# A branch on TensorE in front of the down step of the late expert tiles

## The chip, the core and the metric

One core of one Trainium2 chip runs the whole program. The metric is the device time of one execution, in microseconds. Its engines are TensorE (PE in the profile; PEld is its loading of stationary operands), VectorE (DVE), ScalarE (ACT), GpSimd (POOL) and SyncE (SP). Each engine has a sequencer of its own (PEldq, ACTq and so on in the rows), which takes the instructions of that engine in program order, hands products and vector work on to the engine and carries out register loads, branches and waits on semaphores itself.

## What is computed

```python
X = rfft(x, axis=1)                       # x: (8, 2496, 256)
Yr = Xr @ w_r - Xi @ w_i + b_r ; Yi = Xr @ w_i + Xi @ w_r + b_i
Y = softshrink(Yr, 0.01) + 1j * softshrink(Yi, 0.01)
y = irfft(Y, axis=1).reshape(19968, 256)
logits = y @ w_gate                        # 8 experts
e = argmax(logits) ; g = softmax(logits)[e]
out[token] = g * (relu(y[token] @ w1[e]) @ w2[e])      # w1[e]: 256 x 1024, w2[e]: 1024 x 256
```

Each of the 19,968 tokens goes to one expert. With the inputs of the reference the eight experts get 2254, 2696, 2453, 2444, 2626, 2443, 2081 and 2971 tokens; this is counted from the reference on its own inputs, and is no reading of a trace.

## The kernel before

The first part of the program (the transforms, the mixing, the routing) is not touched. Each routed token is written into a DRAM buffer, `xs_dram`, in which every expert has its own stretch of rows. The second part takes the tokens in tiles of 256 rows (`TT`) of one expert. `tab0`, made when a good half of the tokens is routed, names the first 20 tiles (`EARLY`); `tab1`, made at the end by `table(1)`, names the others: expert by expert, all tiles that this expert still has. The tokens of an expert fill whole tiles only by chance, so an expert's last tile is moved back until it ends with the expert's last row. Its first rows then repeat rows of the tile before. How many they are is `lap`, and `table(1)` makes from it `drop`, which for each late tile and each of its 256 rows is 0, or a large number for a repeated row; added to the row's place in the output it puts that row out of bounds, and it is not written. All 256 rows of the tile are computed nevertheless.

`experts_rest` calls `step(t)` for the tiles 7 to 81, one after the other, with `up(t)` and `down(t)`:

- `up`: hidden layer of the tile, transposed, 1024 x 256, in four groups `ph` (`f2`). Every fp32 product is made of three in the rounded type fp32r: high times high, low times high, high times low. That is 48 products of 128 x 128 by 256 columns (L1143). ACT makes `hh` (relu, rounded, L1148) and DVE `hl` (what the rounding left, L1149) from each group.
- `down`: output of the tile in two halves `h` of 128 rows, each with its own bank `po` of PSUM. `product(..., wide=True)` is hh against the 512 columns of w2's high and low part (L1183, 8 for each half), `wide=False` is hl against the 256 columns of the high part (L1185, 8 for each half). In tiles 7 to 80 all 16 wide ones come first, the halves in turn, then the 16 narrow ones, the halves in turn; in tile 81 (`final`) one half follows the other.
- `give(h)`: ACT scales the low part (`part`, L1189), DVE adds it up to `o` (L1190), POOL scatters the 128 rows to the output (L1192).

`split1(t+1)` and `split2(t+1)` load a flag from the table into registers of ACT and DVE, and where the next tile has another expert, a branch on these two engines makes the high and low parts of the new w1 (L1075, L1076) and w2 (L1081, L1082). The other engines meet such a branch only as a jump from one block of the program to the next (UNCONDITIONAL_BRANCH). `experts_rest` starts with a register load on all engines (`live`, L1243) and ends with a branch of all engines on it (L1247), which decides on three more tiles; with these inputs they are not needed.

The order on ACT and DVE is that of the code; on PE it is as stated above. The instructions of a tile are written out for every tile, so PE's program is a straight line of some 170 instructions a tile, a product and the load of its stationary operand being two.

Of the kernel before, what the change touches and what calls it, by code (L numbers as in the profile page):

```python
# [13 lines left out]
I32 = mybir.dt.int32  # L14
AF = mybir.ActivationFunctionType
ALU = mybir.AluOpType
# [13 lines left out]
TT = 256  # L30
# [3 lines left out]
EARLY = 20  # L34
# [66 lines left out]
class Kernel:  # L101
# [41 lines left out]
    def open_inverse(self, st, pst):  # L143
        nc, nb = self.nc, self.nb
        cp = self.cp
        self.ident = cp.tile([128, 128], F32, name="ident")
        make_identity(nc, self.ident)
        self.carry_b = cp.tile([117, E], BF16, name="carry_b")
        self.base = cp.tile([128, E], F32, name="base")
        nc.vector.memset(self.carry_b, 0.0)  # L150
        self.ones_b = cp.tile([117, 128], BF16, name="ones_b")
        nc.vector.memset(self.ones_b, 1.0)
        self.unit = cp.tile([128, E], F32, name="unit")
        nc.vector.memset(self.unit, 1.0)
        self.used = cp.tile([128, E], F32, name="used")
        nc.vector.memset(self.used, 0.0)
        self.tabs = [cp.tile([1, 4, n], I32, name=f"tab{i}") for i, n in enumerate((EARLY + 4, self.nt - EARLY + 1))]
        self.drop = cp.tile([128, self.nt - EARLY + 1, 2], I32, name="drop")
        self.tcol = cp.tile([128, 5], F32, name="tcol")

        k = self.k = self.pool(st, "k", 1)
        self.wi = self.pool(st, "wi", 3)
        self.rt = self.pool(st, "rt", 1)
        self.psi = self.pool(pst, "psi", 2, space=PSUM)
        self.wg = k.tile([128, 2, 32], F32, name="wg")
        nc.vector.memset(self.wg, 0.0)
        self.gar = k.tile([120, 117], F32, name="gar")
        self.gh = k.tile([120, 128], F32R, name="gh")[:, 0:117]
        self.gl = k.tile([120, 128], F32R, name="gl")[:, 0:117]
        self.ids = k.tile([117, nb, G], I32, name="ids")  # L170
        self.score = k.tile([117, G, E], F32, name="score")
        self.ltri = k.tile([117, 117], BF16, name="ltri")
        self.hot = k.tile([117, 3, GH * E], F32, name="hot")
        self.ltri_f = self.hot.rearrange("p i n -> p (i n)")[:, 0:117]
        self.rank = k.tile([117, E, GH], BF16, name="rank")
        self.keep = k.tile([117, E, GH], F32, name="keep")
        self.ex = k.tile([117, GH, E + 1], F32, name="ex")
        self.mark = k.tile([1, 1], F32, name="mark")
        self.zf = [k.tile([128, 5288], F32, name=f"z{i}") for i in range(2)]
        self.skip(k, 32)  # L180
        self.zs = [z[:, 0:5280].rearrange("p (c n a) -> p c n a", c=2, n=66) for z in self.zf]
# [710 lines left out]
    def table(self, last):  # L892
        nc, rt = self.nc, self.rt
# [5 lines left out]
        for _ in range(6 if last else 0):  # L899
            yield "wait"  # L900
        p = self.psi.tile([128, 512], F32, tag="yo", name="pn")
# [6 lines left out]
                                op0=ALU.add, op1=ALU.mult)  # L908
# [29 lines left out]
        if not last:  # L938
            nc.vector.tensor_scalar(out=st0, in0=st0, scalar1=-1.0, scalar2=float(self.early),
                                    op0=ALU.mult, op1=ALU.add)  # L940
# [19 lines left out]
        p = self.psi.tile([128, 512], F32, tag="yo", name="pq")  # L960
# [5 lines left out]
        if last:  # L966
            lap = rt.tile([128, 128], F32, name="lap")
            nc.vector.tensor_copy(lap, fin[:, 3:4].broadcast_to((128, 128)))
            for _ in range(7):
                yield  # L970
            p = self.psi.tile([128, 512], F32, tag="yo", name="pl")
            nc.tensor.matmul(p[:, 0:128], lap, self.ident, start=True, stop=True)
            for h in range(2):
                nc.vector.tensor_scalar(out=self.drop[:, :, h], in0=p[:, 0:self.drop.shape[1]], scalar1=tcol[:, 3 + h:4 + h],
                                        scalar2=float(OOB), op0=ALU.is_gt, op1=ALU.mult)

# [181 lines left out]
    def down(self, t):  # L1160
        tc, nc = self.tc, self.nc
        hh, hl = self.hs.pop(t)
        w2 = self.h2
        xr = self.xrs.pop(t)
        if t >= self.early:
            row = self.w2p.tile([128, 2], I32, tag="row", name="row", bufs=2)
            nc.vector.tensor_tensor(out=row, in0=xr.bitcast(I32)[:, :, 1], in1=self.drop[:, t - self.early, :],
                                    op=ALU.add)
            at = [row[:, h:h + 1] for h in range(2)]
        else:  # L1170
            at = [xr.bitcast(I32)[:, h, 1:2] for h in range(2)]
        o = self.w2p.tile([128, 2, D], F32, tag="o", name="o", bufs=2)
        if t == self.early:
            self.skip(self.w2p, 160)

        def bank():
            return (self.psb.tile([128, 512], F32, tag="o", name="po") if self.psb else
                    self.psi.tile([128, 512], F32, tag="u", name="po", bufs=4))

        def product(p, h, f, wide):  # L1180
            hs = slice(h * 128, (h + 1) * 128)
            if wide:
                nc.tensor.matmul(p, hh[:, f, hs], w2[:, f].rearrange("p a d -> p (a d)"), start=f == 0, stop=False)  # L1183
            else:
                nc.tensor.matmul(p[:, :D], hl[:, f, hs], w2[:, f, 0, :], start=False, stop=f == 7)  # L1185

        def give(p, h):
            part = self.w2p.tile([128, D], F32, tag="part", name="part", bufs=2)
            nc.scalar.activation(part, p[:, D:], AF.Copy, scale=xr[:, h, 0:1])  # L1189
            nc.vector.scalar_tensor_tensor(out=o[:, h, :], in0=p[:, :D], scalar=xr[:, h, 0:1], in1=part,  # L1190
                                           op0=ALU.mult, op1=ALU.add)
            i = nc.gpsimd.indirect_dma_start(  # L1192
                out=self.out[:, :], out_offset=bass.IndirectOffsetOnAxis(ap=at[h], axis=0),
                in_=o[:, h, :], in_offset=None, bounds_check=self.ntok - 1, oob_is_err=False)
            if t or h:
                tc.declare_no_dep(i.ins, group="out", reason="every token is in one tile only")
            tc.add_to_no_dep_group("out", i.ins)

        if self.psb and t < self.final:
            ps = [bank() for _ in range(2)]  # L1200
            for wide in (True, False):
                for f in range(8):
                    for h in range(2):
                        product(ps[h], h, f, wide)
                if wide:
                    self.split1(t + 1)
                    yield
            for h in range(2):
                give(ps[h], h)
            yield  # L1210
            return
        for h in range(2):
            p = bank()
            for wide in (True, False):
                for f in range(8):
                    product(p, h, f, wide)
                if wide and t < 2:
                    yield
            if not h:
                self.split1(t + 1)  # L1220
            give(p, h)
            yield

    def step(self, t):
        if t + 4 <= self.nt - RARE:
            self.load(t + 4)
        yield from self.up(t, self.upright(t + 1))
        yield from self.down(t)
# [50 lines left out]
```

## Time and profile before

| | us |
|---|---|
| median of 3 runs (lowest, highest) | 1471.36 (1469.13, 1471.93) |
| the profiled execution | 1460.86 |
| its span, first to last instruction | 1459.1 |
| PE busy in the span | 1435.5 |
| DVE, ACT, POOL busy | 926.3, 769.0, 475.0 |

The profile is of one execution, which took 10.5 us less than the median of the runs without a profile. Matmuls are pipelined: the next one starts long before the one before is reported as ended, so what a product costs in a stream is the distance from start to start. The sequencers' instructions are not counted as busy; for an instruction that waits or is late, the reader looks at its start.

### The profile page before, as it was taken

Reading aid. Unit: us, or ns where it says so; the run is one execution under the profiler, and the core shown is the slowest. Engines: PE = TensorE matmul, PEld = TensorE weight load, DVE = VectorE, ACT = ScalarE, POOL = GpSimd, SP = SyncE. Lnnn points to the kernel's source line nnn. Section 1 sums busy time; section 2 is a strip of 40 time slices with the busy share of each in tenths; the row PEclk is TensorE's granted clock in tenths of the full one; section 3 lists DMA queues with packets and bytes.
Section 4 is the critical chain, followed back from the end, with each engine's and each line's share of the span. In section 5 each row is a group of like instructions: output and inputs, shape, how many; then the busy total and the mean of one; then the engine's idle time right before and its main releaser. Section 6 shows DMA issues by size and latency. Waiting matters only on the chain. (4 is left out here: it accounts for less than half of the span.)

```text
span 1459.1 us, 34933 instructions
## 1 busy us (share of the span) xinstructions
PE 1435.5 (98%) x10547; PEld 1311.2 (90%) x10548; DVE 926.3 (63%) x1959; ACT 769.0 (53%) x1540; POOL 475.0 (33%) x586
## 2 busy tenths in 40 slices
PE   8999999999999999999999999999999999999997
PEld 4889898898989878899999999999999999999996
DVE  3788898988998886555565545464445445445443
ACT  2688787787877764443444434343434334334332
POOL 2042566657574454334311111111111111111121
PEclk9999999999999999999999999999999999999999
DMA  7875565656554333444342323233223223232210
GB/s 200 239 229 137 144 177 162 171 162 180 163 155 147 83 98 92 106 125 118 96 117 74 101 59 99 72 87 81 68 55 97 49 56 99 48 85 68 48 50 21
DMA packets 193733, 161.20 MB, mean 110 GB/s; under 512 B 127847, under 2 KB 164367, under 8 KB 193308
## 3 DMA queue, kind: packets, MB, share of 16 engines
q1 hardware_dynamic: 173364, 112.58, 30.7%
q0 software_dynamic: 20160, 46.20, 9.3%
q8 instruction: 87, 1.43, 0.4%
q14 instruction: 122, 1.00, 0.2%
HBM read 241.20 MB, written 66.37 MB: 211 GB/s over the span
## 5 line engine op out<-in xcount | busy, mean ns | idle before, releaser
L1143 PE MATMUL ph<-xh,h 128*128 128x256 f32 x1312 | 363.0, 277 | 0.0
L1143 PE MATMUL ph<-xl,h 128*128 128x256 f32 x1312 | 362.7, 276 | 0.0
L1143 PE MATMUL ph<-xh,l 128*128 128x256 f32 x1312 | 362.7, 276 | 0.0
L1183 PE MATMUL po<-h,hh 128*128 128x512 f32 x1312 | 313.6, 390 | 0.8 <-DVE h L1082 0.5
L1192 POOL DMA_INDIRECT out<-o,row x124 | 121.7, 981 | 556.7 <-DVE o L1190 534.4
L1149 DVE SCALAR_TENSOR_TENSOR hl<-ph,hh 128x512 fp32r<-128x512 f32 x328 | 226.0, 689 | 109.2 <-ACT hh L1148 94.6
L1183 PEld LDWEIGHTS po<-h,hh 128*128 128x128 f32 x1312 | 239.4, 188 | 47.3 <-ACTq L1087 1.5
L1148 ACT ACTIVATE hh<-ph 128x512 fp32r<-128x512 f32 x328 | 194.0, 599 | 159.0 <-PE ph L1143 120.4
L1190 DVE SCALAR_TENSOR_TENSOR o<-po,xr,part 128x256 f32<-128x256 f32 x156 | 68.7, 480 | 311.8 <-ACT part L1189 309.5
L1189 ACT ACTIVATE part<-po,xr 128x256 f32<-128x256 f32 x156 | 65.9, 471 | 344.9 <-PE po L1185 317.9
L1143 PEld LDWEIGHTS ph<-xh,h 128*128 128x128 f32 x1312 | 246.4, 188 | 0.5 <-issue 0.3
L1143 PEld LDWEIGHTS ph<-xl,h 128*128 128x128 f32 x1312 | 246.5, 188 | 0.0
L1143 PEld LDWEIGHTS ph<-xh,l 128*128 128x128 f32 x1312 | 246.3, 188 | 0.2
L877 POOL DMA_INDIRECT xs_dram<-yb,pos x176 | 177.5, 1009 | 59.7 <-issue 44.7
L1185 PEld LDWEIGHTS po<-h,hl 128*128 128x128 f32 x1312 | 167.0, 188 | 6.9
L1185 PE MATMUL po<-h,hl 128*128 128x256 f32 x1312 | 169.1, 279 | 0.0
L475 DVE SCALAR_TENSOR_TENSOR y<-v,r 64x256 f32<-64x256 f32 x320 | 133.6, 417 | 5.7 <-ACT r L469 0.6
L495 ACT COPY z<-pv 128x256 f32<-128x256 f32 x160 | 93.9, 709 | 0.1
L408 PE MATMUL pb<-bm,t 128*128 128x128 f32 x640 | 88.3, 282 | 4.9 <-DMA t<-spec_dram 4.9
L408 PEld LDWEIGHTS pb<-bm,t 128*128 128x128 f32 x640 | 79.8, 194 | 14.4 <-issue 5.6
L491 PE MATMUL pv<-bi,y 128*128 128x128 f32 x640 | 86.9, 277 | 2.3 <-DVE y L475 2.2
L816 POOL COPY mark<-y 1x1 f32<-1x1 f32 x72 | 25.8, 358 | 193.2 <-DVE y L475 192.5
(209 smaller groups left out, 2464.7 us busy)
## 6 DMA issues: line engine op xcount, KB each, us to landing
r<-moe_w SPq DMA_DIRECT2D x672, 128.0 KB
r<-moe_w SPq DMA_DIRECT2D x166, 512.0 KB
xq<-xs_dram SPq DMA_DIRECT2D x332, 64.0 KB
t<-spec_dram SPq DMA_DIRECT2D x160, 128.0 KB
spec_dram<-ae SPq DMA_DIRECT2D x77, 240.0 KB
x<-x SPq DMA_DIRECT2D x38, 384.0 KB
x<-x SPq DMA_DIRECT2D x38, 84.0 KB
xs_dram<-yb,pos POOLq DMA_INDIRECT x176, 2.9
```

The costliest lines, as they stand in the source:

```text
L408: nc.tensor.matmul(p[:, c, :, kp, :], t[:, kp, c * 128:(c + 1) * 128], self.bm[:, 2 * s + kp, :], start=True, stop=True)
L475: nc.vector.scalar_tensor_tensor(out=y[q * 64:q * 64 + 64, kp, :], in0=u[h, q, :], scalar=LAM, in1=r[h, q, :], op0=ALU.add, op1=ALU.min)
L491: nc.tensor.matmul(p[:, c, kp, :, :], y[:, kp, c * 128:(c + 1) * 128], self.bi[:, 2 * s + kp, :], start=True, stop=True)
L495: nc.scalar.copy(self.zs[b % 2][:, c, 0:NB, 4 * s:4 * s + 4].rearrange("p n a -> p a n"), p[:, c].rearrange("p a r n -> p (a r) n"))
L877: i = nc.gpsimd.indirect_dma_start(out=self.xs[:, :], out_offset=bass.IndirectOffsetOnAxis(ap=pos[:n, g:g + 1], axis=0), in_=y[:n, g, :], ...
L1143: nc.tensor.matmul(p[:, i, :], a[:, c, f * 128:(f + 1) * 128], v[:, c, :], start=m == 0, stop=m == 5)
L1148: nc.scalar.activation(hh[:, s, :], p, AF.Relu)
L1149: nc.vector.scalar_tensor_tensor(out=hl[:, s, :], in0=p, scalar=0.0, in1=hh[:, s, :], op0=ALU.max, op1=ALU.subtract)
L1183: nc.tensor.matmul(p, hh[:, f, hs], w2[:, f].rearrange("p a d -> p (a d)"), start=f == 0, stop=False)
L1185: nc.tensor.matmul(p[:, :D], hl[:, f, hs], w2[:, f, 0, :], start=False, stop=f == 7)
L1190: nc.vector.scalar_tensor_tensor(out=o[:, h, :], in0=p[:, :D], scalar=xr[:, h, 0:1], in1=part, op0=ALU.mult, op1=ALU.add)
L1192: i = nc.gpsimd.indirect_dma_start(out=self.out[:, :], out_offset=bass.IndirectOffsetOnAxis(ap=at[h], axis=0), in_=o[:, h, :], in_offset=N ...
```

## The change

`table(1)` makes one more row, `full`: 1 for a late tile with fewer than 128 repeated rows, else 0. In tiles 20 to 80, `down` loads it into a register of PE and branches. Where it is 1, PE does the same products as before, the narrow ones now half by half. Where it is 0, the whole first half of the tile is repeated rows, which are not written: a single wide product fills the first half's bank with numbers that no one needs, the second half is done, and 7 wide and 8 narrow products of the first half are left out. The 8 narrow products of the second half stand behind the branch, for both. In tiles 7 to 19 and 81 nothing is changed.

```diff
--- before.py
+++ after.py
@@ -156,6 +156,7 @@
         nc.vector.memset(self.used, 0.0)
         self.tabs = [cp.tile([1, 4, n], I32, name=f"tab{i}") for i, n in enumerate((EARLY + 4, self.nt - EARLY + 1))]
         self.drop = cp.tile([128, self.nt - EARLY + 1, 2], I32, name="drop")
+        self.full = cp.tile([1, self.nt - EARLY + 1], I32, name="full")
         self.tcol = cp.tile([128, 5], F32, name="tcol")
 
         k = self.k = self.pool(st, "k", 1)
@@ -973,6 +974,8 @@
             for h in range(2):
                 nc.vector.tensor_scalar(out=self.drop[:, :, h], in0=p[:, 0:self.drop.shape[1]], scalar1=tcol[:, 3 + h:4 + h],
                                         scalar2=float(OOB), op0=ALU.is_gt, op1=ALU.mult)
+            nc.vector.tensor_scalar(out=self.full, in0=p[0:1, 0:self.full.shape[1]], scalar1=float(TT // 2), scalar2=1.0,
+                                    op0=ALU.is_lt, op1=ALU.mult)
 
 
 
@@ -1198,13 +1201,25 @@
 
         if self.psb and t < self.final:
             ps = [bank() for _ in range(2)]
-            for wide in (True, False):
+            if t >= self.early:
+                with self.whole(t) as cmp:
+                    for f in range(8):
+                        for h in range(2):
+                            product(ps[h], h, f, True)
+                    for f in range(8):
+                        product(ps[0], 0, f, False)
+                with cmp.Else():
+                    nc.tensor.matmul(ps[0], hh[:, 0, 0:128], w2[:, 0].rearrange("p a d -> p (a d)"), start=True, stop=True)
+                    for f in range(8):
+                        product(ps[1], 1, f, True)
                 for f in range(8):
-                    for h in range(2):
-                        product(ps[h], h, f, wide)
-                if wide:
-                    self.split1(t + 1)
-                    yield
+                    product(ps[1], 1, f, False)
+            else:
+                for wide in (True, False):
+                    for f in range(8):
+                        for h in range(2):
+                            product(ps[h], h, f, wide)
+            self.split1(t + 1)
             for h in range(2):
                 give(ps[h], h)
             yield
@@ -1220,6 +1235,11 @@
                 self.split1(t + 1)
             give(p, h)
             yield
+
+    def whole(self, t):
+        i = t - self.early
+        return self.tc.If(self.nc.values_load(self.full[0:1, i:i + 1], engines=(mybir.EngineType.PE,),
+                                              min_val=0, max_val=1) > 0)
 
     def step(self, t):
         if t + 4 <= self.nt - RARE:
```

The first place is PE between the last product of `up` and the first of the next `up`, in a tile that takes the branch. Here `po` is the output bank, `ph` a group of the hidden layer, h_8031 and h_8032 are the same buffer, w2's parts, and `full` the new row. Before:

```order
L1143 MATMUL ph<-xl_12753,h_7217 128x256
L1095 UNCONDITIONAL_BRANCH
L1183 MATMUL po<-h_8031,hh 128x512 x16
L1185 MATMUL po<-h_8031,hl 128x256 x16
L1087 UNCONDITIONAL_BRANCH
L1143 MATMUL ph<-xh_12961,h_7217 128x256
```

After, with the line numbers of the changed code:

```order
L1146 MATMUL ph<-xl_12755,h_7218 128x256
L1241 TENSOR_LOAD full
L1241 ISA x2
L1098 UNCONDITIONAL_BRANCH
L1205 COMPARE_AND_BRANCH
L1186 MATMUL po<-h_8032,hh 128x512 x16
L1188 MATMUL po<-h_8032,hl 128x256 x8
L1205 UNCONDITIONAL_BRANCH
L1212 MATMUL po<-h_8032,hh 128x512
L1186 MATMUL po<-h_8032,hh 128x512 x8
L1205 UNCONDITIONAL_BRANCH
L1188 MATMUL po<-h_8032,hl 128x256 x8
```

The 16 narrow products fall into 8 before the jump and 8 behind the branch; a register load, two register instructions and a comparison come in front of the wide products; the four rows from the first L1205 jump to the second are the other side of the branch (9 products), which a tile with `full` = 1 jumps over.

The second place is ACT at the end of a tile, from the last two hidden groups to the branch on a new expert (`tab` is the table, h the high part of w1). Before:

```order
L1114 CAST xh_12752<-xf 128x512
L1148 ACTIVATE hh<-ph 128x512 x2
L1055 TENSOR_LOAD tab_75
L1055 ISA x2
L1087 COMPARE_AND_BRANCH
L1075 CAST h_7217<-r_7215 128x512
L1075 CAST h_7217<-r_7216 128x512
```

After:

```order
L1117 CAST xh_12754<-xf 128x512
L1151 ACTIVATE hh<-ph 128x512 x2
L1058 TENSOR_LOAD tab_75
L1058 ISA x2
L1205 UNCONDITIONAL_BRANCH
L1090 COMPARE_AND_BRANCH
L1078 CAST h_7218<-r_7216 128x512
L1078 CAST h_7218<-r_7217 128x512
```

ACT gets one jump a tile in front of that comparison, and its work stands as before; DVE, POOL and SP get the same one jump a tile, 61 in all on each.

## Rows read from the trace of the kernel before

**Rows 1.** Page, busy time of each engine, share of the span and instructions

```profile
PE 1435.5 (98%) x10547; PEld 1311.2 (90%) x10548; DVE 926.3 (63%) x1959; ACT 769.0 (53%) x1540; POOL 475.0 (33%) x586
```

**Rows 2.** Windows: busy us of each engine (instructions), granted clock, DMA share, GB/s

```profile
core 0: us, PE busy (x) PEld busy (x) DVE busy (x) ACT busy (x) POOL busy (x), PEclk, DMA share, GB/s
...
775.90:1444.43 668.53, 668.53 (x4883) 630.55 (x4881) 334.09 (x607) 263.06 (x485) 119.72 (x122) 1.00 0.27 69
...
1104.67:1115.63 10.96, 10.96 (x83) 10.34 (x81) 8.82 (x17) 6.87 (x14) 1.96 (x2) 1.00 0.53 137
```

**Rows 3.** Timeline of PE in tile 50: start, us, engine, line, operation

```profile
1104.67 3.79 PE L1183 MATMUL po<-h,hh 128*128 128x512 f32 x16
...
1108.29 2.04 PE L1185 MATMUL po<-h,hl 128*128 128x256 f32 x16
...
1110.18 0.28 PE L1143 MATMUL ph<-xh,h 128*128 128x256 f32 x1
...
1115.63 0.61 PE L1183 MATMUL po<-h,hh 128*128 128x512 f32 x2
```

**Rows 4.** Timeline of PE in tile 81, one half after the other

```profile
1444.43 1.97 PE L1183 MATMUL po<-h,hh 128*128 128x512 f32 x8
...
1446.24 1.10 PE L1185 MATMUL po<-h,hl 128*128 128x256 f32 x8
...
1447.18 2.02 PE L1183 MATMUL po<-h,hh 128*128 128x512 f32 x8
```

**Rows 5.** Timelines of ACT (tiles 50, 69) and DVE (tile 50)

```profile
1104.87 0.60 ACT L1148 ACTIVATE hh<-ph 128x512 fp32r<-128x512 f32 x1 [0.76 <-PE ph L1143]
...
1105.66 2.19 ACT L1075 CAST h<-r 128x512 fp32r<-128x512 f32 x4 [0.20 <-DMA xq<-xs_dram]
...
1313.92 2.19 ACT L1075 CAST h<-r 128x512 fp32r<-128x512 f32 x4 [0.21 <-ACT hh L1148]
...
1105.50 0.69 DVE L1149 SCALAR_TENSOR_TENSOR hl<-ph,hh 128x512 fp32r<-128x512 f32 x1
...
1106.34 2.50 DVE L1076 TENSOR_TENSOR l<-r,h 128x512 fp32r<-128x512 f32 x4
```

**Rows 6.** By source line, PE's sequencer (PEldq): duration ns, first and last start; one weight load

```profile
L1243 PEldq TENSOR_LOAD <-tab x1: 486/486/486, 624.8 to 624.8; - x1
...
L1143 PEldq EVENT_SEMAPHORE  x1: 51/51/51, 625.4 to 625.4; - x1
...
L1183 PEldq EVENT_SEMAPHORE  x1: 51/51/51, 1102.6 to 1102.6; - x1
...
1104.55 3.48 PEld L1183 LDWEIGHTS po<-h,hh 128*128 128x128 f32 x16
...
L1143 PEldq EVENT_SEMAPHORE  x2: 51/51/51, 1107.9 to 1110.9; - x2
```

**Rows 7.** The same for ACT's sequencer, and ACT's own work then

```profile
L1055 ACTq TENSOR_LOAD <-tab x1: 279/279/279, 940.5 to 940.5; - x1
...
L1087 ACTq COMPARE_BRANCH  x1: 45/45/45, 941.0 to 941.0; - x1
...
L1087 ACTq EVENT_SEMAPHORE  x1: 17/17/17, 941.2 to 941.2; - x1
...
L1095 ACTq COMPARE_BRANCH  x1: 45/45/45, 935.1 to 935.1; - x1
...
934.95 0.84 ACT L1189 ACTIVATE part<-po,xr 128x256 f32<-128x256 f32 x2 [4.84 <-PE po L1185]
```

**Rows 8.** Program's end: PE's one branch, last products, instruction queue from 1447.5 to 1448

```profile
L1247 PEldq COMPARE_BRANCH  x1: 3352/3352/3352, 1447.0 to 1447.0; - x1
...
L1185 PE MATMUL po<-h,hl x8: 276/280/285, 1449.0 to 1449.9; 128*128 128x256 f32 x8
...
q8 instruction: 1, 0.02, 11.1%
```

**Rows 9.** Timeline of DVE at the second table

```profile
600.78 0.47 DVE L974 TENSOR_SCALAR drop<-pl,tcol 128x66 int32<-128x66 f32 x2
```

## The prediction

> **What bounds the kernel now.** I read the page first: PE is busy for 98% of the span, the next engine, DVE, for 63% [rows 1]. The windows say it of the stage that the change touches: from 775.90 (down of tile 20) to 1444.43 (down of tile 81) PE is busy for all 668.53 us, with a granted clock of 1.00, which is the upper of its two levels, while DVE and ACT are busy for half or less [rows 2]. So here the time is the sum of PE's products and nothing else. The timeline of tile 50 gives their price in a stream, start to start [rows 3]: 16 wide ones from 1104.67 to 1108.29, 3.62 us or 0.226 each; 16 narrow ones from there to 1110.18, 1.89 us or 0.118 each; the 48 products of up from there to 1115.63, 5.45 us or 0.113 each. A tile is 10.96 us, and the second window shows it as all busy [rows 2].
>
> **What the skip saves.** Which tiles are skipped follows from the data. From the counts of tokens, lap is 256 times the number of tiles less the count: 50, 120, 107, 116, 190, 117, 223 and 101 for the experts 0 to 7. Only 190 and 223 reach 128: the last tile of expert 4 and that of expert 6. The other 59 of the 61 tiles get the branch for nothing. The trace shows where the two are. Counting 10.96 us a tile from tile 81, the down at 1104.67 is that of tile 50, and in it ACT splits the w1 of a new expert, at 1105.66; the next but one such split stands at 1313.92 [rows 5], 19 tiles on, and experts 5 and 6 have 10 and 9 tiles. So the skips are in tiles 50 and 69.
>
> A skipped down is 1 + 8 wide and 8 narrow products: 9 x 0.226 + 8 x 0.118 = 2.98 us in place of 5.51, a saving of 2.53 us, or 5.06 us for both. That 8 products in a row to one bank cost no more than in turn is shown by tile 81, where 8 wide ones take 1446.24 - 1444.43 = 1.81 us (0.226 each) and 8 narrow ones 1447.18 - 1446.24 = 0.94 (0.118) [rows 4]; so the new order of the narrow ones is free in the 59 tiles too.
>
> Is PE itself what ends last in the shortened tile? The next up, with the new expert's w1, would start at 1104.67 + 2.98 = 1107.65 in place of 1110.18. It needs the first low part of w1, the first of four DVE operations from 1106.34 (2.50 us for four, so it is done at about 1107.0), the second after three products, at 1108.0 (done at about 1107.6), the other two 24 products later [rows 5]. hh's last group is done at 1104.87 + 0.60 = 1105.5, and hl's last at about 1106.2; the skipped down wants them at 1106.3 and 1107.4 [rows 5]. All of it is covered by 0.2 us or more; if that cover were gone, the price is at most the end of the last DVE operation, 1108.84, less 1107.65, some 1.2 us a skip. I take 0.
>
> **What the branch costs.** For PE's array nothing is added; the question is its sequencer, which has to carry out a register load, two register instructions, a jump and a comparison before it can hand on the first wide product. It runs ahead of the array: the wait in front of that product (L1183) is carried out at 1102.6, and the load for the product starts at 1104.55: 1.95 us ahead, or 17 products. In front of the next up the wait at 1107.9 is 2.2 us ahead of 1110.18 [rows 3, 6]. In the same position, right behind a tile's products, the one register load that PE has now (L1243) starts at 624.8 and takes 486 ns; the wait behind it is at 625.4, 0.6 us after the start, and no work of PE is held up by it [rows 6]. For the other instructions ACT has the nearest rows: from the start of its register load at 940.5 to the first instruction on the far side of a taken branch, at 941.2, 0.7 us pass, of which the load is 279 ns [rows 7]. With PE's own load the chain is 0.5 + 0.4 = 0.9 us. PE's wait takes 51 ns where ACT's takes 17; if all small instructions of PE were three times as slow, the chain would be 0.5 + 3 x 0.4 = 1.7 us. Both ends are below 1.95, so I cost the branch at 0: it is hidden by the 17 products already handed on. Behind it come the wide products, at 0.226 us each twice as long as those of up, so the sequencer gets its lead back within the same down.
>
> [...]
>
> Of a tile that jumps over the other side (some 24 instructions), the jump falls behind 8 narrow products, where the lead is larger still. On ACT, DVE, POOL and SP there is one jump a tile more; ACT and DVE are idle for half of the stage [rows 2], so that I cost it at nothing. The operation that makes `full` has one partition and 66 columns; `drop`, 128 partitions and 66 columns, takes 0.24 us each [rows 9], so 0 to 0.24 us, once, beside PE's work: 0.
>
> **The sum.** Profiled execution: 1460.86 - 5.06 = 1455.8 us, its span 1454.0. The median of the runs stands 10.5 us above the profiled execution; I carry that difference over: 1471.36 - 5.06 = 1466.3 us, 0.34% faster. The measurement can tell about 0.2% from no change, that is 2.9 us, so the gain survives if the 59 idle branches cost less than some 35 ns each.
>
> **Rivals.**
>
> 1. The branch empties PE. The only compare-and-branch that PE has now, behind tile 81, starts at 1447.0 and lasts 3352 ns. It ends just when the last product does, whose start is at 1449.9 and which takes 0.28 us [rows 8]. If the comparison waits there until the array is empty, it does so 61 times. Each costs the 0.28 us of the last product less the 0.113 to the next start, then about 0.15 to the branch's end, 0.1 for the wait and the handing on, and 0.12 between the load and the product (1104.55 to 1104.67 [rows 3, 6]): 0.45 to 0.6 us, 27 to 37 us in all. Less 5, this is 1493 to 1503; I would take 1500. Slower than before from 83 ns a branch on. Against it: ACT's comparison at 935.1 takes 45 ns in the midst of work that runs from 934.95 to 935.79 [rows 7], and the register load and jumps of PE do not wait for the array [rows 6]. And there is another cause for the 3352 ns: a block of instructions (0.02 MB) is fetched after 1447.5, out of turn [rows 8]; that branch jumps over three tiles' program, some 500 instructions, to a place that was not there yet.
>
> [...]
>
> 3. The chain is longer than the lead. If PE's sequencer needs 2.1 to 2.4 us for it, 0.15 to 0.45 us stand open in each of 61 tiles: 9 to 27 us, less 5: 1475 to 1494, say 1483.
>
> 4. The skip does not happen, or the next tile waits as long as was saved: 1471.4.
>
> **How the numbers follow.** Hidden branch, two skips: 0.67. The branch empties PE: 0.12. Jumps that miss: 0.06. Chain too long: 0.11. No skip: 0.04. The forecast is 1466.3; with 2.8 us below it, the distance from the lowest to the highest run shown, the range starts at 1463.5. To hold 8 in 10, it has to take in the missing jumps, no skip and the shorter half of the too long chain: 0.67 + 0.06 + 0.04 + 0.05; it ends at 1483. By its own, the forecast's range is 1463.5 to 1469. Faster by over 0.2%: 0.64 (the hidden case, less a little for scatter and the 0.2 us margins). Within 0.2%: 0.12 (that rest, no skip, most of the missing jumps). Slower: 0.24 (emptied PE, long chain, the worst of the jumps).
>
> **What would show it.** In the profile after, PE busy from tile 20 to tile 81 without a gap, that stretch 5.1 us shorter; tiles of 10.96 us, but 8.43 us for tiles 50 and 69, with 9 wide and 8 narrow products. On PE's sequencer, 61 comparisons of 0.1 us or so, and the wait in front of the wide products still ahead of them, by about 1 us. [...] I am wrong if PE has idle time of more than 0.08 us a tile there, or if no tile is short.

## The result and the profile of the changed kernel

| | before | changed |
|---|---|---|
| median of 4 runs (lowest, highest), us | 1470.95 (1469.13, 1471.93) | 1489.23 (1486.20, 1490.06) |
| ratio, 95% interval | | 1.0122 (1.0104 to 1.0140) |
| the profiled execution, us (its span) | 1460.86 (1459.1) | 1490.06 (1488.2) |

The changed kernel is 18.3 us slower; 5 us faster was forecast, and the time lies above the range. The profiled execution of before was 10 us under its own median, that of the changed kernel is not, so the two are compared stage by stage and not by their spans. What sets two executions of the same work apart lies ahead of this stage: in the profile of before, the down step of tile 7 starts at 633.39, in that of e3 below, which took 1468.81 us and has the same tiles of 10.96 us from there on, at 641.30. Its cause is not shown.

The page of the changed kernel still shows PE as what bounds it, as in [rows 1]:

```profile
PE 1455.8 (98%) x10517; PEld 1330.6 (89%) x10518; DVE 930.9 (63%) x1960; ACT 765.3 (51%) x1540; POOL 478.1 (32%) x586
```

The next fence is the windows view of the changed kernel (busy us of each engine with the number of its instructions, granted clock, DMA share, GB/s): from the down step of tile 20 to that of tile 81, one tile with the branch, tile 50, and tile 51.

```profile
core 0: us, PE busy (x) PEld busy (x) DVE busy (x) ACT busy (x) POOL busy (x), PEclk, DMA share, GB/s
792.03:1473.53 681.50, 680.41 (x4853) 641.58 (x4852) 339.37 (x607) 258.93 (x485) 120.56 (x122) 1.00 0.27 68
1095.15:1106.38 11.23, 11.23 (x82) 10.60 (x81) 5.00 (x10) 3.75 (x7) 1.96 (x2) 1.00 0.22 50
1128.83:1138.20 9.37, 8.86 (x68) 8.29 (x66) 7.07 (x14) 6.35 (x13) 2.32 (x2) 1.00 0.44 130
1138.20:1150.43 12.23, 11.65 (x80) 10.61 (x81) 7.56 (x14) 5.18 (x10) 1.97 (x2) 1.00 0.25 57
```

In [rows 2] the stage took 668.53 us and a tile 10.96, all busy. Now the stage takes 681.50, 12.97 more, with PE idle for only 1.09 of them, all of that in the tiles around the first skip. An ordinary tile takes 11.23 us and PE is busy for all of it, at the same granted clock of 1.00 (the only other level in the two traces is 0.50, as from 28.0 to 34.8 us in before), with the same products. So PE does not wait longer; it takes longer for the same work. The timeline of PE (start, us, line, operation) shows which work:

```profile
1095.15 3.80 PE L1186 MATMUL po<-h,hh 128*128 128x512 f32 x16
1098.79 2.05 PE L1188 MATMUL po<-h,hl 128*128 128x256 f32 x16
1100.68 0.28 PE L1146 MATMUL ph<-xh,h 128*128 128x256 f32 x1
...
1106.38 0.86 PE L1186 MATMUL po<-h,hh 128*128 128x512 f32 x3
```

From start to start, the 16 wide products take 3.64 us (3.62 in [rows 3]), the 16 narrow ones 1.89 (1.89), and the 48 products of up take 5.70 (5.45): 0.1188 us each in place of 0.1135. Nothing in the diff touches up. It is slow in tiles 7 to 19 as well, which have no branch: their laps (from down to down) are 11.23 to 11.25 us too. From the down of tile 7 to that of tile 81 there are 74 laps; at about 0.265 us each that is 19.6 us, and the two skips give back 3.3 (below), which leaves 16.3. The traces show 16.4: 827.47 us (646.06 to 1473.53) in place of 811.04 (633.39 to 1444.43). The tiles 1 to 6 in front of them hardly differ, 71.5 us and 71.2 in all. So 16.4 of the 18.3 us have a place; the other 1.9 have none, and the interval of the ratio (15.3 to 20.6 us) does not ask for one.

Everything that the prediction said of the branch is there. PE's sequencer in the tile above, from the rows by source line (duration ns, first and last start):

```profile
L1241 PEldq TENSOR_LOAD <-full x1: 304/304/304, 1104.3 to 1104.3; - x1
L1241 PEldq FUSED_REGOPS  x1: 146/146/146, 1104.7 to 1104.7; - x1
L1205 PEldq COMPARE_BRANCH  x2: 65/117/169, 1105.0 to 1108.0; - x2
L1186 PEldq EVENT_SEMAPHORE  x4: 51/51/51, 1105.1 to 1105.8; - x4
```

From the start of the register load, 1104.3, to the first instruction of the full side, 1105.1, 0.8 us pass, and the first wide product starts at 1106.38, 1.2 us later. Over the whole run, the same view:

```profile
L1205 PEldq COMPARE_BRANCH  x120: 65/169/347, 790.7 to 1463.9; - x120
L1241 PEldq TENSOR_LOAD <-full x61: 295/303/469, 789.9 to 1460.2; - x61
```

These are 61 comparisons and 59 jumps over the other side. The comparisons take 65 ns in 57 tiles, 71 and 93 in two, 207 and 347 in tiles 50 and 69; the jumps take 169 to 312. No comparison lasts until PE's array is empty, and nothing comes near the 3352 ns of the far branch [rows 8].

The skips happened in tiles 50 and 69. PE's timeline around the first:

```profile
1128.83 0.40 PE L1212 MATMUL po<-h,hh 128*128 128x512 f32 x1
1129.07 1.98 PE L1186 MATMUL po<-h,hh 128*128 128x512 f32 x8
1130.89 1.10 PE L1188 MATMUL po<-h,hl 128*128 128x256 f32 x8
1131.83 0.28 PE L1146 MATMUL ph<-xh,h 128*128 128x256 f32 x1
...
1138.20 2.11 PE L1186 MATMUL po<-h,hh 128*128 128x512 f32 x8 [0.51 <-ACT hh L1151]
1140.88 2.13 PE L1186 MATMUL po<-h,hh 128*128 128x512 f32 x8 [0.58 <-ACT hh L1151]
```

The down step itself is 3.00 us, as forecast (2.98). But the next down waits twice for hh. Tiles 50 and 51 together take 9.37 + 12.23 = 21.60 us, only 0.85 less than two ordinary tiles; tiles 69 and 70 take 8.69 + 11.26 us, 2.50 less. Both together are 3.3 us, not 5.06.

### The profile page after: what moved, and what is told of

It reads as the page before. It is cut to its first block, busy times and chain, and to the rows that moved or that the text cites. A ratio compares the mean times of both kernels' runs of the same rounds, so it can differ in the third digit from the quotient of the medians.

```text
span 1488.2 us, 35179 instructions
## 1 busy us (share of the span) xinstructions
PE 1455.8 (98%) x10517; PEld 1330.6 (89%) x10518; DVE 930.9 (63%) x1960; ACT 765.3 (51%) x1540; POOL 478.1 (32%) x586
## 5 line engine op out<-in xcount | busy, mean ns | idle before, releaser
L1146 PE MATMUL ph<-xl,h 128*128 128x256 f32 x1312 | 370.3, 282 | 0.0
L1146 PE MATMUL ph<-xh,h 128*128 128x256 f32 x1312 | 370.3, 282 | 0.0
L1146 PE MATMUL ph<-xh,l 128*128 128x256 f32 x1312 | 369.9, 282 | 0.0
L1193 DVE SCALAR_TENSOR_TENSOR o<-po,xr,part 128x256 f32<-128x256 f32 x156 | 74.1, 483 | 290.0 <-ACT part L1192 260.7
L1192 ACT ACTIVATE part<-po,xr 128x256 f32<-128x256 f32 x156 | 72.4, 474 | 322.9 <-PE po L1188 279.7
```

The source lines that it names most:

```text
L1146: nc.tensor.matmul(p[:, i, :], a[:, c, f * 128:(f + 1) * 128], v[:, c, :], start=m == 0, stop=m == 5)
```

## The experiments

What made up slower? Between before and the changed kernel, up's products have the same instructions, but not the same addresses. The new tile `full` takes 264 bytes of every partition (288 with rounding) in the pool `cp`, and every tile allocated later on the left side of SBUF, h1 and l1 among them, stands 288 bytes higher. `skip` in the code reserves bytes of padding that nothing uses: 544 of them stand in front of r1, h1 and l1, others in front of w2's parts, xh, hh and hl. The theory: placement makes up slow, and the branch is free. The rival: the branch slows the supply of instructions to PE.

**The row's bytes alone (e1), and only w1's tiles moved (e4).**

```diff
 self.drop = cp.tile([128, self.nt - EARLY + 1, 2], I32, name="drop")
+self.skip(cp, 264)                      # e1, on the kernel before
 ...
-self.skip(k2, 544)
+self.skip(k2, 832)                      # e4, on the kernel before
```

> The kernel before, with 264 bytes of SBUF reserved where the changed kernel has its new row `full`; nothing is computed there, nothing branches. All that it does is to move every later tile on the left side of SBUF by 288 bytes, as in the changed kernel. Placement theory (the up products are slower since h1 and l1 have moved): 82 tiles x 48 products x (0.1188 - 0.1135) us = 20.9 us, and 0.02 us a tile for the wide ones, 1.6 us: 1493 us. Branch theory (the 61 branches slow PE's supply of instructions): 1471 us, as before.

> The kernel before, with the padding in front of w1's tiles 832 instead of 544 bytes: only r1, h1, l1 and the first tiles' rows (xq, xi) move by 288 bytes, the tiles of the first part stay. If h1 and l1 are what counts: up products of 0.1188 us, 1471 + 22 = 1493 us. If it is the operands of the first part that count: 1471 us and products of 0.1135 us.

Measured: 1491.05 us (ratio 1.0141, 1.0124 to 1.0158) and 1491.14 us (1.0142, 1.0125 to 1.0159). PE's timeline of a tile of e4:

```profile
996.89 0.28 PE L1143 MATMUL ph<-xh,h 128*128 128x256 f32 x1
...
1002.60 3.80 PE L1183 MATMUL po<-h,hh 128*128 128x512 f32 x16
1006.24 2.05 PE L1185 MATMUL po<-h,hl 128*128 128x256 f32 x16
1008.12 0.28 PE L1143 MATMUL ph<-xh,h 128*128 128x256 f32 x1
```

The down step has the numbers of the changed kernel, 3.64 and 1.88; up takes 5.71 us, a tile 11.23. There is no branch in either kernel, no operation is added, and the whole loss is there. In e4 the tiles of the first part stand where they were; what moved is w1's tiles (r1, h1, l1) and the rows of the tiles 0 to 3. The laps behind tile 7 use w1's tiles alone of these, so it is their place that costs the 20 us.

**The changed kernel with all other tiles in their old places (e2), and the same without a skip (e3).** The row goes into the padding:

```diff
-self.full = cp.tile([1, self.nt - EARLY + 1], I32, name="full")
 ...
-self.skip(k2, 544)
+self.full = k2.tile([1, self.nt - EARLY + 1], I32, name="full")
+self.skip(k2, 256)
 ...
-... scalar1=float(TT // 2), scalar2=1.0, ...     # e3 only: full is 1 everywhere
+... scalar1=float(TT), scalar2=1.0, ...
```

> The changed kernel, with its row `full` moved into the 544 bytes of padding in front of w1's tiles (288 of them are taken, 256 are left), so that every other tile has its address of before. Placement theory: tiles of 10.96 us again, 8.43 us for the two skipped ones, 1470.95 - 5.06 = 1465.9 us. Branch theory: 1489 us as the changed kernel, tiles of 11.23 us.

> As the placed version, but the bound in `full` is 256 repeated rows instead of 128, so that all 61 tiles take the full side: the branch alone. Placement theory with a hidden branch: 1471 us, no tile shorter than 10.96 us. Branch theory: 1489 + 5 = 1494 us.

Measured: e2 1469.64 us (0.9989, 0.9979 to 0.9999), e3 1470.41 us (1.0002, 0.9993 to 1.0011). The windows of one tile of e3 and the row of its comparisons:

```profile
1101.66:1112.62 10.96, 10.96 (x83) 10.34 (x81) 4.94 (x10) 3.75 (x7) 1.96 (x2) 1.00 0.51 142
```

```profile
L1205 PEldq COMPARE_BRANCH  x122: 65/130/309, 782.6 to 1443.0; - x122
```

With 61 comparisons and 61 jumps, every lap from tile 16 to tile 81 of e3 is 10.96 us: the branch costs nothing that a lap shows. Together with e1 this settles the 20 us. But e2 gains only about 1.6 us (0.1 to 3.1, just clear of the noise) and not 5. Its laps say where the rest is: 9.41 and 11.97 around tile 50 (0.54 us less than two tiles), 8.63 and 11.11 around tile 69 (2.18 less), all others 10.96: 2.7 us. PE at tile 50 of e2, and ACT in the same stretch:

```profile
1115.04 0.39 PE L1212 MATMUL po<-h,hh 128*128 128x512 f32 x1
...
1118.02 0.28 PE L1146 MATMUL ph<-xh,h 128*128 128x256 f32 x1
...
1124.45 2.10 PE L1186 MATMUL po<-h,hh 128*128 128x512 f32 x8 [0.61 <-ACT hh L1151]
1127.13 2.11 PE L1186 MATMUL po<-h,hh 128*128 128x512 f32 x8 [0.57 <-ACT hh L1151]
```

```profile
1118.14 0.82 ACT L1192 ACTIVATE part<-po,xr 128x256 f32<-128x256 f32 x2
1120.60 1.14 ACT L1084 CAST h<-r 128x512 fp32r<-128x512 f32 x2 [1.64 <-DMA r<-moe_w]
1122.76 1.14 ACT L1084 CAST h<-r 128x512 fp32r<-128x512 f32 x2 [1.02 <-DMA r<-moe_w]
1123.81 1.08 ACT L1151 ACTIVATE hh<-ph 128x512 fp32r<-128x512 f32 x2
```

ACT is through with the skipped tile's output at about 1119.0 and then waits twice for the new expert's w2, until 1120.60 and 1122.76. Only behind the split of w2 does it come to hh of the next tile, at 1123.81, and PE's wide products wait for that. The second half of w2 is used 7.7 us after the start of the shortened down. In before, ACT does the same four splits without a wait, from 6.4 us after the start of the down (1104.67) on:

```profile
1110.31 0.84 ACT L1189 ACTIVATE part<-po,xr 128x256 f32<-128x256 f32 x2 [2.46 <-issue]
1111.04 2.18 ACT L1081 CAST h<-r 128x512 fp32r<-128x512 f32 x4
1113.11 1.09 ACT L1148 ACTIVATE hh<-ph 128x512 fp32r<-128x512 f32 x2
```

The two transfers of w2 are issued at the same time behind the start of the down, 1.8 and 2.5 us in before, 1.7 and 2.5 in e2. So the load had next to no time to spare, and most of PE's 2.5 us were spent waiting for it.

Not all of them: in both shortened tiles of e2, where every address is that of before, up is slow. At tile 69 nothing waits in it:

```profile
1322.74 0.39 PE L1212 MATMUL po<-h,hh 128*128 128x512 f32 x1
...
1325.72 0.28 PE L1146 MATMUL ph<-xh,h 128*128 128x256 f32 x1
...
1331.37 3.94 PE L1186 MATMUL po<-h,hh 128*128 128x512 f32 x16
```

The down is 2.98 us, but up takes 5.65, not 5.45; that is the 0.20 us by which the lap of 8.63 misses 8.43. At tile 50 up takes 6.43, of which 0.8 is the wait for hh and 0.20 again the rate. So 0.40 us of the two skips went to a slower up, and the rest of the loss, 1.9 us, to hh behind the split of w2: 1.8 at tile 50, 0.15 at tile 70.

**The w2 load issued earlier (e5),** on e2: in front of the loads of w1 behind the split of w1, instead of behind the split of w2.

```diff
 def split1(self, t):
     ...
+    if self.psb:
+        self.ahead = t + 1
+        self.weights(t + 1, 2)
     self.weights(t + 1, 1)
 ...
 def split2(self, t, qs=range(4)):
     ...
-    if 3 in qs:
+    if 3 in qs and self.ahead != t + 1:
         self.weights(t + 1, 2)
```

> The placed version, with the loads of the next expert's w2 issued one half tile earlier (in front of the loads of w1, behind the split of w1, instead of behind the split of w2). Only valid for tables in which no two late tiles in a row have a new expert, as here. Theory of the late w2 load (in the placed version the skipped down of tile 50 and the tile after it take 9.41 + 11.97 us, 0.54 us less than two whole tiles instead of 2.53, because ACT waits until 1122.76 for w2 and hh stands behind that on ACT): with the load in time, 8.43 + 10.96 us, and 2 us less than the placed version, 1468 us by the median. Rival (the split itself, 2.2 us of ACT and 2.5 us of DVE, comes too soon after w1's, wherever the load is): 9.0 us or more and 11 to 12 us as in the placed version, and the same time as that, 1469.6 us.

Measured: 1468.33 us (0.9991, 0.9980 to 1.0003), which can't be told from e2. The trace can: the laps are now 9.03 and 10.99 around tile 50 and 8.63 and 10.96 around tile 69, 1.90 and 2.33 us less than two tiles, so 4.2 of the 5.06 us are there. But two earlier laps, at 739.5 and 772.90, are 11.44 and 12.48 us. ACT's timeline at the second says why, and its third row, from tile 50, shows the same wait there:

```profile
777.12 0.62 ACT L1079 CAST h<-r 128x512 fp32r<-128x512 f32 x1 [3.42 <-DMA r<-moe_w]
778.87 1.66 ACT L1079 CAST h<-r 128x512 fp32r<-128x512 f32 x3 [1.13 <-DMA r<-moe_w]
...
1116.53 1.66 ACT L1079 CAST h<-r 128x512 fp32r<-128x512 f32 x3 [0.72 <-DMA r<-moe_w]
```

L1079 is the split of w1, whose loads now stand behind those of w2 on the same queue. The theory of the late load holds for the tile behind the skip: PE no longer waits for hh there, the 16 wide products take 3.66 us in place of 4.63. The rival (the split comes too soon wherever the load is) named the 9.03 and the unchanged time, but not their cause: the 9.03 comes from up, which takes 6.05 us, 0.4 of them for the late split of w1 and 0.20 for the slower rate. The two earlier laps pay back 2.0 of the 4.2 us.

**Which placement?** Thirteen more kernels are the kernel before with other paddings, nothing else (each edit changes or removes a few `skip`; hl stands in front of hh in three; g1 is on e2). Each has its own place of the tiles, given as the address modulo 512; the times are from start to start, as read above, to about 0.01 us, from one trace of each. All but g1 and g2 ran only once, and single executions of one kernel differ by more than 10 us (the kernel before took 1460.07 in one round and 1473.76 in another), so the lap is the number to read.

| kernel | h1, l1 | xh, xl | w2 | hh | hl | up, 48 | wide, 16 | narrow, 16 | lap |
|---|---|---|---|---|---|---|---|---|---|
| before, e2, e3 | 0 | 192 | 64 | 64 | 256 | 5.45 | 3.62 | 1.89 | 10.96 |
| changed, e1, e4 | 288 | 192 | 64 | 64 | 256 | 5.70 | 3.64 | 1.89 | 11.23 |
| d1 | 32 | 192 | 64 | 0 | 0 | 5.70 | 3.66 | 1.89 | 11.25 |
| d2 | 64 | 192 | 64 | 64 | 64 | 5.70 | 3.63 | 1.91 | 11.24 |
| d4 | 0 | 224 | 64 | 64 | 256 | 5.68 | 3.63 | 1.88 | 11.19 |
| f1 | 32 | 224 | 64 | 64 | 384 | 5.44 | 3.65 | 1.89 | 10.98 |
| f2 | 0 | 192 | 64 | 384 | 384 | 5.46 | 3.72 | 1.89 | 11.07 |
| f3 | 0 | 192 | 192 | 0 | 0 | 5.44 | 3.73 | 1.82 | 10.99 |
| f4 (512 bytes lower) | 0 | 192 | 64 | 64 | 256 | 5.45 | 3.62 | 1.89 | 10.96 |
| g1, g2 (hl in front) | 0 | 192 | 192 | 192 | 0 | 5.66 | 3.65 | 1.89 | 11.19 |
| k1 (hl in front) | 0 | 192 | 64 | 64 | 0 | 5.45 | 3.63 | 1.88 | 10.96 |
| k2 | 0 | 192 | 192 | 192 | 192 | 5.65 | 3.66 | 1.91 | 11.22 |
| m1 | 0 | 192 | 64 | 192 | 256 | 5.65 | 3.72 | 1.89 | 11.26 |
| m2 | 0 | 192 | 192 | 64 | 256 | 5.66, 5.44 | 3.71, 3.72 | 1.88, 1.82 | 11.25, 10.98 |

> The kernel before, r1, h1 and l1 moved by only 32 bytes (h1 and l1 then stand at 32 behind a multiple of 512 and of 64), and hl moved back from 256 to 0 behind a multiple of 512, hh from 64 to 0. If a stationary operand off a multiple of 64 bytes is what costs: up products 0.1188 us, narrow ones 0.118 as before. If it has to be at a multiple of 512: up 0.1188 us, narrow 0.1135, wide a little below 0.226. If only the distance of 288 bytes does it: up 0.1135 us.

> The kernel before, r1, h1 and l1 moved by 64 bytes, hl moved from 256 to 64 behind a multiple of 512. Multiple of 64 wanted: up products 0.1135 us, narrow 0.118. Multiple of 512 wanted: up 0.1188 us, narrow 0.118.

> The kernel before, w1's tiles where they were, and the other operand of the up products, xh and xl, moved by 32 bytes (from 192 to 224 behind a multiple of 512). If only the stationary operand's address counts: up products 0.1135 us. If any operand off a multiple of 64 costs, or the two addresses against each other: 0.1188 us.

All three were slow (1491.49, 1491.09 and 1488.22 us). So a multiple of 64 seems not to be enough (d2, up 5.70 us), 512 does not concern the stationary operand alone (d4 moves only the other one, up 5.68), and narrow products with hl at 0 did not become faster (d1, 1.89 us for 16). d1 and d2 are no clean tests of w1's place: d1 moved hh and hl as well, d2 hl, and m1 below shows that hh alone can make up slow. What was tried next was the distance between a product's two operands, 192 for up.

> The kernel before, w1's tiles moved by 32 bytes and xh, xl by 32 as well, so that both operands of up are off a multiple of 64 but as far from each other as before (192 behind a multiple of 512); and hl moved from 256 to 384 behind a multiple of 512, so that w2's parts (at 64) stand 192 behind it, as xh stands behind h1 in the kernel before. If the distance between the two operands counts: up products 0.1135 us and narrow ones 0.1135 (from 0.118). If the addresses themselves count (0 and 192): up 0.118 us or more, narrow 0.118.

> The kernel before, r1, h1 and l1 moved by -512 bytes. If only the address modulo 512 counts: up products 0.1135 us, 1471 us. If the place counts in a longer period: up 0.118 us or more, 1491 us.

> The kernel before, hh and hl both at 384 behind a multiple of 512, so that w2's parts (at 64) stand 192 behind both. [...] Address theory: 0.118 and 0.226 us as before, 1471 us.

> The kernel before, w2's parts moved to 192 and hh and hl to 0 behind a multiple of 512: both the addresses and the distance of up's operands in the kernel before. [...] If the down products' price has nothing to do with the addresses: 0.118 and 0.226 us, 1471 us.

For up, f1 and f4 agree with the distance: both operands moved by 32, 5.44 us; h1 and l1 moved by 512, 5.45. (One tile of f4 is an exception, see below.) For down it fell: in f2, at the distance of 192, the narrow products stay at 1.89 and the wide ones get slower (3.72), and in f3 the narrow ones do fall to 1.82, but the wide ones rise to 3.73. No placement shows wide products below the 0.226 us each of before (3.62 us for 16). As laps, f2 is 0.11 us worse than before and f3 0.03.

> The placed version of the changed kernel, and the down step's operands placed by what the looks showed: w2's parts and hh at 192, hl at 0 behind a multiple of 512 (distance 0 for the wide products, 192 for the narrow ones; hl stands in front of hh for that). Distance theory, each kind of product with its own distance: wide 0.226, narrow 0.1135, up 0.1135 us, a tile 10.89 us instead of 10.96, 82 x 0.07 = 5.9 us less than the placed version: 1463.7 us. If the narrow products' gain is taken back by the wide ones, as with hh and hl both at 0: 1469.6 us.

> The kernel before with the same places of w2's parts, hh and hl: no branch, no skip. Distance theory: 1470.8 - 5.9 = 1465 us. Branch and skip are then worth what this kernel takes more than the one with them: 1.3 to 2.7 us if the late load of w2 takes back most of it again (2.7 us is what the two short tiles and their followers save in the trace of the placed version), 5.06 us if the timing of the placed version was short by chance.

Measured: g1 1481.77 us (1.0073, 1.0059 to 1.0087), g2 1487.96 us (1.0115, 1.0100 to 1.0131). Both theories are wrong: up is slow (5.66 us), with its own operands where they were before. Beside each other they say of branch and skip that g1 is 6.2 us faster by the medians; its trace has ordinary laps of 11.19 and 11.20 as g2 has, and 9.26, 12.17, 8.66 and 11.19 around the skips, 3.5 us less than four ordinary ones. The other 2.7 us have no place in the laps from tile 7 on; by the two intervals the 6.2 are uncertain by about 3 us (an estimate), so they need none.

> The kernel before with hl in front of hh in SBUF; hh still at 64 and w2's parts at 64, hl at 0 behind a multiple of 512. If the order (the place in SBUF at large) of hh and hl makes the up products slow: 0.118 us, tiles of 11.2 us. If it was the addresses of w2 and hh modulo 512 (192): up 0.1135 us, tiles of 10.96 us.

> The kernel before with w2's parts, hh and hl all at 192 behind a multiple of 512, hh in front of hl as before. If the order of hh and hl makes the up products slow: up 0.1135 us here, tiles of 10.96 us. If the 192 of w2 and hh does it: up 0.118 us, tiles of 11.2 us. In both cases the wide products, at distance 0, should take 0.226 us, if the distance sets their price.

> The kernel before with hh alone moved by 128 bytes, from 64 to 192 behind a multiple of 512. If the place to which ACT writes hh while PE reads xh and xl (at 192) makes up's products slow: up 0.118 us, tiles of 11.2 us or more. If only the operands that a product itself reads set its price: up 0.1135 us; the wide products, then at distance -128, may change.

> The kernel before with w2's parts alone moved by 128 bytes, from 64 to 192 behind a multiple of 512 (and with them xf, which PE doesn't read). If w2's place makes up's products slow: up 0.118 us, tiles of 11.2 us or more; if only a product's own operands count: up 0.1135 us, and the wide and narrow ones, then at distance 128 and -64, may change.

k1 is as fast as before (laps of 10.96, 1471.33 us), k2 is slow (1493.15 us): not the order, the addresses. m1 moves hh alone and nothing that up reads, and up is slow (5.65 us; 1484.95 us in all), as its first theory said, and as in g1, g2 and k2, which have hh at 192 too. But that theory cannot be the whole: e4, d2 and d4 are slow with hh at 64, and in m1 the loss is not where ACT writes hh. The 1st, 13th, 25th and 37th product of an up start at 1001.13, 1002.54, 1003.95 and 1005.37, the next down at 1006.78: 1.41 us for each twelve (1.36 in before), though ACT's first write of hh in this up starts only at 1002.74. In e4 it is 1.42 or 1.43 for each twelve. The products are slower all along, not in bursts. m2 moves w2 alone, and does something else: it alternates. Three successive tiles of m2 in PE's timeline:

```profile
1005.02 2.05 PE L1183 MATMUL po<-h,hl 128*128 128x256 f32 x16
1006.90 0.28 PE L1141 MATMUL ph<-xh,h 128*128 128x256 f32 x1
...
1012.56 3.88 PE L1181 MATMUL po<-h,hh 128*128 128x512 f32 x16
1016.28 1.98 PE L1183 MATMUL po<-h,hl 128*128 128x256 f32 x16
1018.10 0.28 PE L1141 MATMUL ph<-xh,h 128*128 128x256 f32 x1
...
1023.54 3.87 PE L1181 MATMUL po<-h,hh 128*128 128x512 f32 x16
1027.25 2.05 PE L1183 MATMUL po<-h,hl 128*128 128x256 f32 x16
1029.13 0.28 PE L1141 MATMUL ph<-xh,h 128*128 128x256 f32 x1
```

The narrow products take 1.88, 1.82, 1.88 us, and so on to the end; the up behind 1.88 takes 5.66, the one behind 1.82 takes 5.44. The narrow ones read hl and w2 only, which have one buffer each, at the same addresses in every tile. So the price of a product is not a function of its own operands' addresses alone. Two more places show it: the shortened tiles of e2, whose up takes 5.65 us at the addresses of before, and one tile of f4, whose neighbours all take 10.96:

```profile
785.58 3.86 PE L1183 MATMUL po<-h,hh 128*128 128x512 f32 x16
...
791.16 0.28 PE L1143 MATMUL ph<-xh,h 128*128 128x256 f32 x1
...
796.82 3.79 PE L1183 MATMUL po<-h,hh 128*128 128x512 f32 x16
```

Its wide products take 0.07 us longer than usual, and the up behind them 5.66. That something is carried on from one group of products to the next would fit all three; what it is, these runs do not show. xh and xl have two buffers, 2048 bytes apart, used in turn, which may be what sets the alternation of m2 going; this was not tested.

By the lap none of these placements beats the 10.96 us of before, which e2 has. e2 is ahead of both kernels, by about 1.3 us in the medians against before.

## Why the prediction was wrong

**What bounds the kernel** was right: PE, before without a gap, after with 1.09 us of idle time in the whole stage.

**"For PE's array nothing is added"** is the step that failed. It looked for added instructions, and for `full` it priced the DVE operation (0 to 0.24 us; the trace shows 204 ns, once). It did not price the row's 264 bytes. The prices 0.226, 0.118 and 0.113 were taken from [rows 3] as properties of the products; they hold for the products at these places of the tiles, and the change moved tiles: 0.1135 became 0.1188 in every up, in the same stream with other addresses. e1, which adds nothing but the bytes, has the whole loss: 0.25 us a tile in up and 0.02 in the wide products, 19.8 us from tile 7 to tile 81 (830.8 in place of 811.0). The hint was in the kernel: paddings of 32 to 544 bytes with no use of their own. None of the rivals had this in it, so the range had no reason to reach 1489.

**The branch at nothing** was right, and close in its parts: the chain was put at 0.9 to 1.7 us and took 0.8, and the lead is still 1.2 us, as forecast "by about 1 us". e3 measures the whole: 1.0002 (0.9993 to 1.0011).

**The saving of 5.06 us** was right for the down step (3.00 us, 2.98 in e2, in place of 5.51 in before) and wrong for the path. The step "Is PE itself what ends last in the shortened tile?" went through w1's splits, hh and hl up to the next up, and stopped there. In [rows 5] the w1 split is covered, and so it was: up does not wait for it in either skip of e2. The next tile's down, however, wants a new w2 too, which is loaded while the shortened tile runs. Its load is issued at the same time whether PE skips or not (1.8 and 2.5 us behind the start of the down in before, 1.7 and 2.5 in e2, at tile 50), and "the price is at most" 1.2 us a skip was exceeded at tile 50: 2.0 us in e2, 1.8 of them the wait for hh behind the split of w2. At tile 69 the load was issued 0.9 us earlier in the tile, and 2.2 of 2.53 us were kept. The other 0.20 us at either skip are the failed step once more: 0.113 us a product of up did not hold behind a shortened down, even with every address as before.

**The rivals.** The emptied array: none. In the first tile of the changed kernel shown above, the comparison starts at 1105.0 and the last product of up at 1106.25, for 0.29 us; a comparison that waits for its end would take 1.5 us (an estimate from these rows), and the longest is 347 ns. Jumps that miss, which have 0.06 of the chances and a part of the range: no run shows a near jump that waits for its instructions, the 59 take 169 to 312 ns. Of the far branch the trace of before shows that the instruction queue q8 brings 0.02 MB while it lasts, at 1447.9, out of its turn (50 times from 600 to 1440 us, one every 16.8 us, the last at 1437.8); whether the branch waits for this is not shown. The chain longer than the lead: no, 0.8 us, with 1.2 to spare. The last, "the next tile waits as long as was saved", is most of what happened at tile 50: 2.0 of 2.53 us.

**Had the row been put into the padding,** the forecast of 1466.3 would have met 1469.64 us: the right sign, and 3.3 us short, of which the laps show 2.3: 1.9 the wait for w2, 0.4 the slower up. The other 1.0 is within the scatter of the runs.

## What to carry to other kernels

A new tile moves the tiles that are allocated behind it in its pool and in later pools: here 264 bytes moved them by 288. Where TensorE streams without a gap, compare the addresses of the operands before and after a change, and keep them, for instance by taking the new bytes out of padding; else a change of 288 bytes may cost 4.6% of a stream of products that it never touches, as here. And where work is cut out of a chain, follow the chain through the next round: a load that was only just in time takes back what was saved, here 1.8 of 2.53 us at tile 50.

## What the runs showed of the hardware

- The same 48 products of 256 columns take 5.44 to 5.46 or 5.65 to 5.71 us by the placement of SBUF tiles alone, and behind the down step of tile 7 no ordinary tile that was read, in the 14 placements, took anything in between. Tile 7's own up did: 5.53 us in before, the first 18 products 0.118 us from start to start, the others 0.114. The granted clock is 1.00 in both (before and changed).
- Moving w1's parts by 512 bytes leaves up at 5.45 us (f4, but for one tile of 5.66), moving them by 288 makes it 5.70 (e4), and moving xh and xl by 32 makes it 5.68 (d4); with both operands of up moved by 32 it stays at 5.44 (f1). Moving hh by 128, which up does not read, makes up 5.65 (m1). Where up is slow, it is so evenly over its 48 products: 1.41 us for each twelve in m1, 1.42 or 1.43 in e4, 1.36 in before.
- The rate is not fixed by the addresses of a product's operands: in m2 the narrow products alternate between 1.82 and 1.88 us from tile to tile with unchanged operand addresses, and the up behind them between 5.44 and 5.66; at the addresses of before, up takes 5.65 us behind the shortened downs of e2. Why is open; a theory by the distance of two operands fits up in d1 to f4, and fails for down (f2: wide 3.72 us, narrow 1.89) and for up in g1, k2 and m1 (5.65 to 5.66).
- A register load, two register instructions and a comparison on PE cost 0.8 us of its sequencer and none of its array where it runs 1.2 us ahead, as here: the laps of e3, with 61 of them, are 10.96 us as before. In the changed kernel the load takes 295 to 469 ns, the comparison 65 ns in 57 of 61 tiles and 207 and 347 where it is taken, the jump over some 24 instructions 169 to 312 ns.
